# Half a weight chunk kept resident in place of a second output-tail buffer, in a streamed recurrent attention kernel

## The chip, the cores and the metric

The kernel runs on one core of one Trainium2 chip. The metric is the device time of one execution in microseconds. A time given here is the median of the fast runs of one kernel. A ratio is the mean time of one kernel's fast runs over the mean of the other's fast runs of the same rounds on the same chip, so it is not quite the ratio of the medians quoted beside it. All runs of this study were in the fast state. The kernel before was run anew beside each group of experiments, with medians from 2193 to 2199 us.

Names used below: PE is the matmul engine (TensorE), DVE the vector, ACT the scalar and POOL the general engine; SP issues the loads. The granted clock is the share of TensorE's full clock that the profile's records show. "The fill" is the copy of the memory rows into the input of a segment, once per segment.

## The reference, cut to what matters

The program computes two things side by side: a long convolution (part A, not touched here), and an attention with a recurrent memory (part B). Part B goes through 64 segments of 32 rows. Each segment takes eight memory rows from the output of the one before, so the segments cannot overlap.

```python
mem = mem0
for s in range(n_seg):                                   # 64
    h = jnp.concatenate([mem, x[:, s*32:(s+1)*32]], axis=1)
    q, k, v = (jnp.einsum('btd,dhe->bhte', h, W) for W in (Wq, Wk, Wv))
    p = softmax(where(mask, q @ k^T * scale, -1e9))
    o = jnp.einsum('bhte,hed->btd', p @ v, Wo)
    mem = o[:, :M, :]                                    # M = 8
    outs.append(o[:, M:, :])
```

The weights Wq, Wk, Wv and Wo are 64 chunks of [128, 2048] bf16, 512 KB each. The kernel holds only part of them on the chip.

## The kernel before: the parts that matter

43 of the 64 chunks stay resident. 21 are "streamed", two of which are kept in spare PSUM after the first segment, so 19 loads of 512 KB go through a ring of six slots in every segment. A load is issued only when a slot comes free: `done` of a used chunk calls `fetch`.

```python
def fetch():
    if loads:
        s, ch = loads.pop(0)
        live[s, ch] = k, t = slot()
        nc.sync.dma_start(t[:], stream_src(ch))

def done(ch):
    if ch in streamed:
        ...
        free.append(live.pop((now[0], ch))[0])
        ...                      # either a kept chunk is moved into the slot, or
        fetch()
```

The order of work in a segment (cut) is: K, Q and V projections for two groups of heads, scores, softmax, attention, output projection. Then comes the turn: eight rows of the result Y go through a transpose into the input of the next segment.

```python
k0 = Proj(0, 0).run().evac()
q0 = Proj(1, 0).run(4)
...                                        # KT0, QT0, k1
scores(0, QT0, KT0); softmax_a()
q1 = Proj(1, 1).run(4)
...
PT0 = softmax_b()                          # P_pad on DVE, transposed into PT
...
QT1 = one.tile(..., tag="QT"); nc.scalar.copy(QT1[:], transposes(q1))
scores(1, QT1, KT1); softmax_a()
...
out_proj(...)                              # with tail heads on streamed chunks
nc.scalar.copy(Y[:], yacc[:, 0:256])
if tail is not None and not last: tail.run(TURN[0])      # six heads as filler
if not last: fill_mem(pend[s + 1][0], Y)                 # the turn
...
if tail is not None and not last: tail.run(TURN[1])      # four more
```

The "tail" is the output projection of eight more rows per segment. They are collected in OTB for a pair of segments and multiplied together: 32 heads of four matmuls for each pair, then one store YB. A head whose output chunk is streamed has to ride along while that chunk is in the ring ("inline").

Of the kernel before, what the change touches and what calls it, by code (L numbers as in the profile page):

```python
# [9 lines left out]
BF = mybir.dt.bfloat16  # L10
F32 = mybir.dt.float32
# [11 lines left out]
KEPT = {18: "A", 6: "B"}  # L23
TURN = (6, 4)
INLINE = {1: 0, 3: 1, 5: 0, 11: 1, 12: 0, 14: 1}
N2, N3 = 12, 19
# [358 lines left out]
def b_kernel(ctx: ExitStack, tc, x, mem0, Wq, Wk, Wv, Wo, outb, n_seg, run_a):  # L385
    nc = tc.nc
    SEG = 32
    NX = 24
    NB = 2
# [9 lines left out]
    order = []  # L399
# [7 lines left out]
    streamed = set()  # L407
# [13 lines left out]
    def dram_chunk(ch):  # L421
        m, a, g = ch
        return Wo_v[a] if m == 3 else W_v[m][a, g]
# [4 lines left out]
    def stream_src(ch):  # L428
        return WS[ring_order.index(ch), :, 0:2048]
# [186 lines left out]
    one = ctx.enter_context(tc.tile_pool(name="b_one", bufs=1, side="right", reuse_waits="tile"))  # L616
    two = ctx.enter_context(tc.tile_pool(name="b_two", bufs=2, side="right", reuse_waits="tile"))
    ps_acc = ctx.enter_context(tc.tile_pool(name="b_ps_acc", bufs=2, space=PSUM))
# [15 lines left out]
    tacc = SB[:, 200:456]  # L634
# [14 lines left out]
    def slot():  # L649
        k = free.pop(0)  # L650
        t = ring.tile([128, 2048], BF, tag=f"wring{k}", name="wring")
        return k, t

    def fetch():
        if loads:
            s, ch = loads.pop(0)
            live[s, ch] = k, t = slot()
            nc.sync.dma_start(t[:], stream_src(ch))

# [12 lines left out]
    def pieces(ch):  # L672
        if ch in res:
            return [(0, 2048, res[ch])]
        t = live[now[0], ch][1]
        if kept.get(ch) == "B" and now[0] > 0:
            return [(0, 768, WB[:]), (768, 2048, t[:, 768:2048])]
        return [(0, 2048, t[:])]
# [7 lines left out]
    def done(ch):  # L686
        if ch in streamed:
# [7 lines left out]
            else:  # L695
                fetch()

    P_pad = one.tile([128, 5, 64], BF, name="P_pad")
    nc.vector.memset(P_pad[:], 0.0)

# [17 lines left out]
    with tc.manual_schedule():  # L718
# [17 lines left out]
        class Tail:  # L736


            def __init__(self, OTB, b, acc=None):
                self.OTB, self.b, self.acc = OTB, b, tacc if acc is None else acc  # L740
                self.seeded = acc is None
                self.left = list(range(32))
                nc.vector.memset(self.acc, 0.0)  # L743

            def head(self, h, w):
                g, c, i = h // 16, (h % 16) // 4, h % 4
                first = len(self.left) == 32
                self.left.remove(h)
                for dq in range(4):
                    o = (h % 2) * 1024 + dq * 256  # L750
                    for x, y, r in columns(w, o, o + 256):
                        nc.tensor.matmul(self.acc[32 * dq:32 * dq + W, x - o:y - o],  # L752
                                         lhsT=self.OTB[:, c, 4 * g + i, :], rhs=r,
                                         start=first and not self.seeded, stop=not self.left,
                                         skip_group_check=True, tile_position=(0, 32 * dq))
                if not self.left:
                    self.store()
# [5 lines left out]
            def store(self):  # L763
                YB = one.tile([128, 256], BF, tag="QT", name="YB")
                nc.vector.tensor_copy(YB[:], self.acc)  # L765
                for dq in range(4):
                    nc.gpsimd.dma_start(  # L767
                        bass.AP(outb.tensor, outb.offset + (SEG * NB * self.b + NX) * 2048 + 256 * dq,
                                [[2048 * SEG, NB], [2048, 8], [1, 256]]), YB[32 * dq:32 * dq + W, :])

        OTB = tail = own = None
        for s in range(n_seg):
            b, j = s // NB, s % NB
# [59 lines left out]

            def softmax_a():
                mx = two.tile([128, 5], F32, tag="mx", name="mx")
                nc.vector.tensor_reduce(out=mx[:], in_=S, op=ALU.max, axis=AX.X)  # L836
                nc.vector.tensor_tensor(out=S, in0=S, in1=mx[:].unsqueeze(2).to_broadcast([128, 5, 40]),
                                        op=ALU.subtract)
                nc.scalar.activation(S, S, ACT.Exp, scale=scale)

            def softmax_b():
                ssum = two.tile([128, 5], F32, tag="ssum", name="ssum")
                nc.vector.tensor_reduce(out=ssum[:], in_=S, op=ALU.add, axis=AX.X)  # L843
# [38 lines left out]
            def out_proj(hps, OT):  # L882
                for hp in hps:
                    ch = (3, hp, 0)
                    w = pieces(ch)
                    for hh in range(2):
                        h = 2 * hp + hh
                        g, c, i = h // 16, (h % 16) // 4, h % 4
                        for dq in range(4):
                            o = hh * 1024 + dq * 256  # L890
                            for x, y, r in columns(w, o, o + 256):
                                nc.tensor.matmul(yacc[32 * dq:32 * dq + 32, x - o:y - o], lhsT=OT[:, c, i, :],  # L892
                                                 rhs=r, start=(h == 0 and x == o), stop=(h == 31),
                                                 tile_position=(0, 32 * dq))
                    if tail is not None and 2 * hp in tail.left and (ch in streamed or last):
                        if last or INLINE[hp] == j:
                            tail.head(2 * hp, w)
                            tail.head(2 * hp + 1, w)
                    if own is not None and ch in streamed:
                        own.head(2 * hp, w)  # L900
                        own.head(2 * hp + 1, w)
                    done(ch)

            k0 = Proj(0, 0).run().evac()
            q0 = Proj(1, 0).run(4)
            KT0 = keys(0)
            last_queries(0)
            nc.vector.tensor_copy(KT0[:, :, :, 0:32], transposes(k0))  # L908
            q0 = q0.run(4).evac()
            k1 = Proj(0, 1).run(4)  # L910
            QT0 = one.tile([128, 4, 4, 32], BF, tag="QT", name="QT")
            nc.vector.tensor_copy(QT0[:], transposes(q0))
            k1 = k1.run(4).evac()
            scores(0, QT0, KT0)
            softmax_a()
            q1 = Proj(1, 1).run(4)
            KT1 = keys(1)
            last_queries(1)
            nc.scalar.copy(KT1[:, :, :, 0:32], transposes(k1))
            PT0 = softmax_b()  # L920
            q1 = q1.run(4).evac()
# [4 lines left out]
            scores(1, QT1, KT1)  # L926
            softmax_a()
            pv1 = Proj(2, 1).run(4)
            if j == 0:
                OTB_new = one.tile([128, 4, 8, 8 * NB], BF, tag=f"OTB{b % 2}", name="OTB")  # L930
                OTB = OTB_new
            attend(0, PT0, V0)
            OT0 = evac_o(0)
            PT1 = softmax_b()
            pv1.run(4)
# [3 lines left out]
            yacc = ps_acc.tile([128, 512], F32, tag="acc", name="yacc")  # L939
            if last:  # L940
                own = Tail(OTB, b, ps_acc.tile([128, 512], F32, tag="acc", name="own_acc")[:, 0:256])
            out_proj(range(0, 5), OT0)
# [5 lines left out]
            nc.scalar.copy(Y[:], yacc[:, 0:256])  # L948
            if j == NB - 1 and not last:
                tail = Tail(OTB, b)  # L950
            if tail is not None and not last:
                tail.run(TURN[0])
            if not last:
                fill_mem(pend[s + 1][0], Y)
            nc.gpsimd.dma_start(bass.AP(outb.tensor, outb.offset + SEG * s * 2048, [[256, 4], [2048, 32], [1, 256]]), Y[:])
            if tail is not None and not last:
                tail.run(TURN[1])
            if last:
                own.run(32)

# [69 lines left out]
```

## Time and profile before

Three runs gave 2200.15 us (2194.8 to 2205.34).

| Quantity | Value | Where from |
|---|---|---|
| Span of the profile | 2198.0 us | page |
| Rate in the segments | 383 to 393 GB/s | table of stretches |
| Granted TensorE clock, whole span | 0.965 | list of cores |

The lines themselves stand in the prediction. The table of stretches gives busy time for each engine, then the granted clock, the share of time the 16 DMA engines were busy with packets, and what they moved.

### The profile page before, as it was taken

The numbers are of one execution on the slowest core, as the hardware profiler recorded it, in microseconds if no ns is written. First come the engines' busy times: TensorE is split into PE (matmuls) and PEld (weight loads), VectorE is DVE, ScalarE is ACT, GpSimd is POOL, SyncE is SP. The second block draws the span as 40 slices with busy tenths as digits, with TensorE's granted clock in tenths as the row PEclk, the third lists the DMA queues.
The fourth block names the chain that finished last, engine by engine and source line by source line (L and its number), as shares of the span: only waits on it lengthen the run. The fifth ranks groups of instructions, "written<-read, shape, count | busy, mean of one in ns | idle before, by whom it ended". The sixth has DMA issues, their size and how long they took to land. (4 is left out here: it accounts for less than half of the span.)

```text
span 2198.0 us, 81500 instructions
## 1 busy us (share of the span) xinstructions
PE 1721.9 (78%) x35607; PEld 927.7 (42%) x35636; DVE 884.2 (40%) x2702; ACT 638.6 (29%) x1118; POOL 412.2 (19%) x1103
## 2 busy tenths in 40 slices
PE   4679975957777788878888888887887878888886
PEld 2233332424444444444444444444444444444444
DVE  8827853123333333333333333333333333333332
ACT  5845530112222222222222222222222222222222
POOL 5004331001111112111111111111111211211111
PEclk9889997879999999999999999999999999999999
DMA  9989989899999999999999999999999999999997
GB/s 322 345 291 342 318 238 325 275 346 390 386 380 378 381 374 390 385 378 395 391 392 395 391 393 393 392 397 365 396 392 387 394 390 376 388 392 388 390 385 273
DMA packets 294286, 807.80 MB, mean 368 GB/s; under 512 B 84940, under 2 KB 84972, under 8 KB 293927
## 3 DMA queue, kind: packets, MB, share of 16 engines
q1 hardware_dynamic: 263592, 738.36, 89.0%
q0 software_dynamic: 23536, 50.51, 6.8%
q10 hardware_dynamic: 6800, 13.72, 1.7%
q8 instruction: 279, 4.57, 0.9%
q14 instruction: 79, 0.65, 0.1%
HBM read 743.06 MB, written 62.39 MB: 366 GB/s over the span
## 5 line engine op out<-in xcount | busy, mean ns | idle before, releaser
L806 PEld LDWEIGHTS <-rec 128*32 128x32 bf16 x12351 | 324.2, 96 | 471.6 <-issue 255.0
L806 PE MATMUL acc<-wring,rec 128*32 128x512 bf16 (+1 forms) x3777 | 374.7, 385 | 136.0 <-DMA wring<-WS 122.1
L815 ACT CAST qkv_sb<-acc 128x512 bf16<-128x512 f32 x384 | 224.8, 585 | 676.2 <-PE acc L806 645.7
L806 PE MATMUL acc<-Wres,rec 128*32 128x512 bf16 x4864 | 394.9, 383 | 1.5 <-issue 1.4
L892 PEld LDWEIGHTS <-OT 128*32 128x32 bf16 x8192 | 217.8, 96 | 178.1 <-issue 151.6
L892 PE MATMUL yacc<-Wlate,OT 128*32 128x256 bf16 x5120 | 221.8, 274 | 13.0 <-issue 11.9
L892 PE MATMUL yacc<-wring,OT 128*32 128x256 bf16 x3072 | 153.9, 276 | 98.5 <-DMA wring<-WS 59.0
L806 PE MATMUL acc<-Wmid,rec 128*32 128x512 bf16 x3072 | 226.1, 383 | 0.5 <-issue 0.5
L752 PEld LDWEIGHTS <-OTB 128*16 128x16 bf16 x4096 | 104.5, 89 | 103.9 <-issue 94.0
L878 ACT CAST OT<-OTp 128x512 bf16<-128x512 f32 x128 | 74.9, 585 | 241.4 <-PE OTp L870 241.3
L707 POOL DMA_DIRECT2D rec<-REC x64 | 37.4, 584 | 566.6 <-issue 268.9
L908 DVE COPY KT<-tps 128x512 bf16<-128x512 bf16 x64 | 27.2, 424 | 289.1 <-PE tps L821 289.1
L879 DVE CAST OTB<-OTp 128x128 bf16<-128x128 f32 x128 | 37.3, 291 | 258.6 <-ACT OT L878 258.6
L647 DVE TENSOR_SCALAR wring<-OTp 128x384 int32<-128x384 int32 x126 | 112.2, 890 | 61.5 <-PE acc L806 54.2
L752 PE MATMUL SB<-Wlate,OTB 128*16 128x256 bf16 x2480 | 98.0, 277 | 35.4 <-DVE SB L743 19.3
L782 POOL COPY KT<-rec 128x128 bf16<-128x128 bf16 x128 | 38.6, 302 | 439.2 <-PE SB L830 430.9
L836 DVE TENSOR_REDUCE mx<-SB 128x5 f32<-128x200 f32 x128 | 47.1, 368 | 182.8 <-PE SB L830 182.8
L767 POOL DMA_DIRECT2D out_dram<-YB x128 | 73.1, 578 | 236.4 <-DVE YB L765 212.9
L752 PE MATMUL SB<-wring,OTB 128*16 128x256 bf16 x1488 | 78.8, 274 | 36.5 <-DVE SB L731 30.8
L821 PE MATMUL tps<-ident,qkv_sb 128*128 128x128 bf16 x1024 | 101.2, 221 | 7.8 <-DVE wring L647 0.2
L821 PEld LDWEIGHTS <-qkv_sb 128*128 128x128 bf16 x1024 | 62.7, 97 | 104.7 <-ACT qkv_sb L815 64.4
L556 PE MATMUL kb_ps<-XBT,pw 128*128 128x512 bf16 x314 | 87.7, 400 | 9.3 <-ACT XBT L512 7.6
(214 smaller groups left out, 2300.8 us busy)
## 6 DMA issues: line engine op xcount, KB each, us to landing
wring<-WS SPq DMA_DIRECT2D x1218, 512.0 KB, 7.3
rec<-REC POOLq DMA_DIRECT2D x64, 192.0 KB, 6.0
SK<-s_sb SPq DMA_DIRECT2D x16, 512.0 KB, 4.8
SU<-s_sb SPq DMA_DIRECT2D x16, 512.0 KB, 4.6
Ug<-SU SPq DMA_DIRECT2D x32, 256.0 KB, 6.1
Kg<-SK ACTq DMA_DIRECT2D x32, 256.0 KB, 5.5
REC<-stage SPq DMA_DIRECT2D x4, 2048.0 KB, 15.2
SZ<-zs SPq DMA_DIRECT2D x31, 256.0 KB, 3.0
```

The lines of the kernel that those rows point to most:

```text
L556: nc.tensor.matmul(ps[:], lhsT=ws[kc][:, hl * 128:(hl + 1) * 128], rhs=XBT[:, kc].rearrange("p s t -> p (s t)"), start=(kc == 0), stop=(kc ...
L647: nc.vector.tensor_scalar(out=dst, in0=src, scalar1=0, scalar2=None, op0=ALU.bitwise_or)
L707: nc.gpsimd.dma_start(rec[:], REC[:, s, :])
L752: nc.tensor.matmul(self.acc[32 * dq:32 * dq + W, x - o:y - o], lhsT=self.OTB[:, c, 4 * g + i, :], rhs=r, start=first and not self.seeded, ...
L767: nc.gpsimd.dma_start(bass.AP(outb.tensor, outb.offset + (SEG * NB * self.b + NX) * 2048 + 256 * dq, [[2048 * SEG, NB], [2048, 8], [1, 256 ...
L782: nc.gpsimd.tensor_copy(KT[:, :, :, 32:40], KBs[:, 128 * g:128 * g + 128].rearrange("p (c i t) -> p i c t", c=4, i=4))
L806: nc.tensor.matmul(self.acc[32 * c:32 * c + 32, x - 512 * c:y - 512 * c], lhsT=hT[:, kc, :], rhs=r, start=(kc == 0 and x == 512 * c), stop ...
L815: nc.scalar.copy(sb[:], self.acc[:])
L821: nc.tensor.transpose(tp[:, i * 128:(i + 1) * 128], sb[:, i * 128:(i + 1) * 128], ident[:])
L836: nc.vector.tensor_reduce(out=mx[:], in_=S, op=ALU.max, axis=AX.X)
L878: nc.scalar.copy(OT[:], o_view[:, :, :, 0:32])
L892: nc.tensor.matmul(yacc[32 * dq:32 * dq + 32, x - o:y - o], lhsT=OT[:, c, i, :], rhs=r, start=(h == 0 and x == o), stop=(h == 31), tile_po ...
```

## The change

The intent is to stream less. The left half of one K chunk (place 3 of the 64) becomes resident. Its 2 KB per partition come from one OTB buffer instead of two, from single buffers for two small softmax tiles, and from letting P_pad borrow the slots of the transposed Q and K. With one OTB, the tail of a pair must be finished before the next pair writes OTB, so the tail work moves: twelve heads inline in the second segment of each pair, ten as filler there, ten early in the next. YB moves from the slot "QT" to the slot "PT". The core of the diff:

```diff
-TURN = (6, 4)
-INLINE = {1: 0, 3: 1, 5: 0, 11: 1, 12: 0, 14: 1}
+TURN = (4, 6)
+HALF = 3
...
+    half = order[HALF]
+    WH = one.tile([128, 1024], BF, name="WH")
+    nc.gpsimd.dma_start(WH[:], dram_chunk(half)[:, 0:1024])
...
-            nc.sync.dma_start(t[:], stream_src(ch))
+            c = slice(1024 if ch == half else 0, 2048)
+            nc.sync.dma_start(t[:, c], stream_src(ch)[:, c])
...
-    P_pad = one.tile([128, 5, 64], BF, name="P_pad")
-    nc.vector.memset(P_pad[:], 0.0)
...
-                YB = one.tile([128, 256], BF, tag="QT", name="YB")
+                YB = one.tile([128, 256], BF, tag="PT", name="YB")
...
+            def softmax_a(g):
+                P_pad = one.tile([128, 5, 64], BF, tag="KT" if g else "QT", name="P_pad")
+                nc.gpsimd.memset(P_pad[:, 0:4, 32:64], 0.0)
...
-                        if last or INLINE[hp] == j:
+                    if j == NB - 1 and ch in streamed:
...
             k0 = Proj(0, 0).run().evac()
+            more_tail(4)
             q0 = Proj(1, 0).run(4)
+            more_tail(3)
...
             q0 = q0.run(4).evac()
+            more_tail(32)
...
-                OTB_new = one.tile([128, 4, 8, 8 * NB], BF, tag=f"OTB{b % 2}", name="OTB")
+                OTB = one.tile([128, 4, 8, 8 * NB], BF, tag="OTB", name="OTB")
```

More of the change, by code (lines that the diff above doesn't have):

```diff
@@ L616, in b_kernel @@
     one = ctx.enter_context(tc.tile_pool(name="b_one", bufs=1, side="right", reuse_waits="tile"))
-    two = ctx.enter_context(tc.tile_pool(name="b_two", bufs=2, side="right", reuse_waits="tile"))
+    two = ctx.enter_context(tc.tile_pool(name="b_two", bufs=1, side="right", reuse_waits="tile"))
     ps_acc = ctx.enter_context(tc.tile_pool(name="b_ps_acc", bufs=2, space=PSUM))
@@ L675, in pieces @@
         t = live[now[0], ch][1]
+        if ch == half:
+            return [(0, 1024, WH[:]), (1024, 2048, t[:, 1024:2048])]
         if kept.get(ch) == "B" and now[0] > 0:
@@ L736, in b_kernel, with __init__ @@
         class Tail:
-            def __init__(self, OTB, b, acc=None):
-                self.OTB, self.b, self.acc = OTB, b, tacc if acc is None else acc
-                self.seeded = acc is None
+            def __init__(self, OTB, b):
+                self.OTB, self.b, self.acc = OTB, b, tacc
                 self.left = list(range(32))
@@ L746, in head @@
                 g, c, i = h // 16, (h % 16) // 4, h % 4
-                first = len(self.left) == 32
                 self.left.remove(h)
@@ L753, in head @@
                                          lhsT=self.OTB[:, c, 4 * g + i, :], rhs=r,
-                                         start=first and not self.seeded, stop=not self.left,
+                                         start=False, stop=not self.left,
                                          skip_group_check=True, tile_position=(0, 32 * dq))
@@ L769, in store @@
                                 [[2048 * SEG, NB], [2048, 8], [1, 256]]), YB[32 * dq:32 * dq + W, :])
-        OTB = tail = own = None
+        OTB = tail = None
         for s in range(n_seg):
@@ L832, in scores @@
                                          tile_position=(0, 32 * c))
-            def softmax_a():
+            def softmax_a(g):
+                P_pad = one.tile([128, 5, 64], BF, tag="KT" if g else "QT", name="P_pad")
+                nc.gpsimd.memset(P_pad[:, 0:4, 32:64], 0.0)
                 mx = two.tile([128, 5], F32, tag="mx", name="mx")
@@ L839, in softmax_a, with softmax_b @@
                 nc.scalar.activation(S, S, ACT.Exp, scale=scale)
-            def softmax_b():
-                ssum = two.tile([128, 5], F32, tag="ssum", name="ssum")
+                return P_pad
+            def softmax_b(P_pad):
+                ssum = two.tile([128, 5], F32, tag="mx", name="ssum")
                 nc.vector.tensor_reduce(out=ssum[:], in_=S, op=ALU.add, axis=AX.X)
@@ L894, in out_proj, with more_tail @@
                                                  tile_position=(0, 32 * dq))
-                    if tail is not None and 2 * hp in tail.left and (ch in streamed or last):
-                        if last or INLINE[hp] == j:
-                            tail.head(2 * hp, w)
-                            tail.head(2 * hp + 1, w)
-                    if own is not None and ch in streamed:
-                        own.head(2 * hp, w)
-                        own.head(2 * hp + 1, w)
+                    if j == NB - 1 and ch in streamed:
+                        tail.head(2 * hp, w)
+                        tail.head(2 * hp + 1, w)
                     done(ch)
+            def more_tail(n):
+                if tail is not None and j == 0:
+                    tail.run(n)
             k0 = Proj(0, 0).run().evac()
+            more_tail(4)
             q0 = Proj(1, 0).run(4)
+            more_tail(3)
             KT0 = keys(0)
@@ L914, in b_kernel @@
             scores(0, QT0, KT0)
-            softmax_a()
+            P0 = softmax_a(0)
             q1 = Proj(1, 1).run(4)
@@ L919, in b_kernel @@
             nc.scalar.copy(KT1[:, :, :, 0:32], transposes(k1))
-            PT0 = softmax_b()
+            PT0 = softmax_b(P0)
             q1 = q1.run(4).evac()
@@ L926, in b_kernel @@
             scores(1, QT1, KT1)
-            softmax_a()
+            P1 = softmax_a(1)
             pv1 = Proj(2, 1).run(4)
             if j == 0:
-                OTB_new = one.tile([128, 4, 8, 8 * NB], BF, tag=f"OTB{b % 2}", name="OTB")
-                OTB = OTB_new
+                OTB = one.tile([128, 4, 8, 8 * NB], BF, tag="OTB", name="OTB")
             attend(0, PT0, V0)
             OT0 = evac_o(0)
-            PT1 = softmax_b()
+            PT1 = softmax_b(P1)
             pv1.run(4)
@@ L939, in b_kernel @@
             yacc = ps_acc.tile([128, 512], F32, tag="acc", name="yacc")
-            if last:
-                own = Tail(OTB, b, ps_acc.tile([128, 512], F32, tag="acc", name="own_acc")[:, 0:256])
+            if j == NB - 1:
+                tail = Tail(OTB, b)
             out_proj(range(0, 5), OT0)
@@ L948, in b_kernel @@
             nc.scalar.copy(Y[:], yacc[:, 0:256])
-            if j == NB - 1 and not last:
-                tail = Tail(OTB, b)
-            if tail is not None and not last:
+            if j == NB - 1:
                 tail.run(TURN[0])
@@ L955, in b_kernel @@
             nc.gpsimd.dma_start(bass.AP(outb.tensor, outb.offset + SEG * s * 2048, [[256, 4], [2048, 32], [1, 256]]), Y[:])
-            if tail is not None and not last:
-                tail.run(TURN[1])
-            if last:
-                own.run(32)
+            if j == NB - 1:
+                tail.run(32 if last else TURN[1])
 @with_exitstack
```

## The prediction

> **What bounds the kernel now.** I read the page's slices first, then the table of stretches, the chain of waits, the list of waits and a timeline of one segment. The kernel has two stages. Up to about 460 us it does the convolution and preparation; after that come 64 sequential segments, and only those are changed. The fill of the memory rows happens once per segment; its first copy starts at 468.6 us and the last at 2159.1 us, so a segment takes (2159.1 - 468.6) / 63 = 26.83 us. In each segment 19 chunks of 512 KB are streamed into a six-slot ring (1218 loads in all). Two stretches inside the segments, columns: length, busy us (instructions) of PE, PEld, DVE, ACT, POOL, then granted clock, DMA share, GB/s:
>
> ```profile
> 1000.00:1400.00 400.00, 325.72 (x8073) 186.20 (x8069) 146.88 (x529) 104.54 (x198) 72.14 (x227) 1.00 1.02 393
> 1400.00:1800.00 400.00, 324.02 (x7961) 184.95 (x7957) 145.69 (x524) 102.44 (x194) 69.90 (x223) 0.99 1.01 389
> ```
>
> The DMA engines are full (share 1.0) at 389 to 393 GB/s. PE is busy for 81% and idle for (400 - 325.72) / 400 x 26.83 = 5.0 us of a segment. The chain of waits, asked for 1900 to 1965 us, says the same: what releases a load is the slot freed by the matmuls of an earlier load, and most of the chain is the transfer itself.
>
> ```profile
> by line: DMA wring<-WS 86.8%; PE acc L806 6.3%; PE yacc L892 5.9%; DVE wring L647 4.0%; issue 2.3%; PE tps L821 1.2%; PE SB L752 1.0%; DVEq L912 0.1%; PE SB L830 0.1%; PE SB L827 0.1%; DVEq L647 0.0%
> ```
>
> How much room PE has is in the waits (us in total, times, longest). PE waits for the stream 122.1 + 59.0 = 181 us, 2.8 us a segment; the rest of its 5.0 us is latency of softmax, copies and the recurrence.
>
> ```profile
> PE acc L806 <- DMA wring<-WS: 122.1, 276, 2.0
> PE yacc L892 <- DMA wring<-WS: 59.0, 110, 1.6
> PE SB L752 <- DVE SB L731: 30.8, 29, 1.6
> PE SB L752 <- DVE SB L743: 19.3, 28, 0.7
> ```
>
> The buffer between both is in the list of issues (KB, us to landing): a load lands 7.3 us after its issue because some six are in flight, so PE may fall several us behind before the DMA engines run out of requests. The small stores take almost as long[...]:
>
> ```profile
> wring<-WS SPq DMA_DIRECT2D x1218, 512.0 KB, 7.3
> out_dram<-Y POOLq DMA_DIRECT2D x64, 64.0 KB, 6.4
> out_dram<-YB POOLq DMA_DIRECT2D x128, 8.0 KB, 5.0
> ```
>
> [...] the packet records have a median of 162 ns for the 163,712 packets of 4096 B on the ring's queue and 84 ns for those of 2048 B (26,907 on the same queue, all of the first stage), 3.7% more per byte. [...] The trace shows 393 GB/s here[...] and I use the measured rate. [...]
>
> **The change, part by part.**
>
> Half a chunk resident. Columns 0 to 1023 of the fourth K chunk stay in SBUF; the ring fetches only the other half, 128 packets of 2048 B in place of 128 of 4096 B. On 16 engines that is 128 x (162 - 84) ns / 16 = 0.624 us less per segment, 64 x 0.624 = 39.9 us in all. By bytes alone, 262144 B at 393 GB/s would be 0.667 us and 42.7 us; the shorter packet takes the difference back. It is paid once with the resident half's own load, 128 x 84 / 16 = 0.67 us of engine time in the crowded start. Matmul forms do not change, since the cut at 1024 lies between two 512-column matmuls. As the DMA engines set the pace, this part should come through nearly whole: -39 us.
>
> The output tail. A pair of segments still does 32 tail heads with 128 matmuls, about 0.11 us of PE per head at the measured 8 matmuls in 0.22 us. Before: each segment runs six heads inline and ten as filler around the recurrence. After: twelve inline and ten filler in the second segment of a pair, the other ten early in the next segment, where PE waits for transposes or the stream. PE work is moved, not removed. The wait on L743 (19 us) should go, because the accumulator is cleared long before its first matmul; the one on L731 stays, at one segment of each pair. PE is not the bound, so I count 0.
>
> The end. The last segment had two tails: the store of the first held the slot that the second needed, and the program ended 12.6 us after its last Y copy (2185.4 to 2198.0). Now one tail is left; its YB shares a slot with Y and waits for Y's store alone. I estimate -2 us.
>
> P_pad in the Q and K slots. It adds 128 memsets of 128x128 on POOL, about 0.3 us each by the KT copy of that size (302 ns), off the path. It also makes the copy of the second Q wait until softmax has transposed P_pad out of the first Q's slot; in the timeline that was done at 1024.1 us and the copy began at 1025.6 us, so there is 1.5 us of room.
>
> YB in the slot of PT. This is the new cost. YB is now copied about 7.5 us into the first segment of each pair, after the last tail head; four stores of 0.56 us follow on POOL, the last starting 1.7 us later and landing 5.0 us after that: about 14.5 us into the segment. The transposes that fill PT need this slot. Before they began 10.6 us after the fill in this segment:
>
> ```profile
> 1012.99 0.19 DVE L714 COPY rec<-tps 128x64 bf16<-128x64 bf16 x1 [1.20 <-issue]
> 1023.54 0.30 DVE L857 STREAM_TRANSPOSE PT<-P_pad 128x128 bf16<-128x128 bf16 x1
> 1025.60 0.58 ACT L924 COPY QT<-tps 128x512 bf16<-128x512 bf16 x1 [0.94 <-PE tps L821]
> ```
>
> So DVE should stand about 3.5 us for YB's landing in 31 or 32 segments, and PE some 2 to 3 us at the second scores, because the copy of Q waits for P_pad. During that stand about two chunks land, with three or more still on order: the DMA engines stay fed. PE must then make it up: of the 2.8 us of waiting for the stream, 0.6 goes to the faster stream and at most 3.3 / 2 = 1.65 us a segment on average to this stall, which leaves some 0.5 us. That is thin, so I charge 5 us, about 0.15 us per pair, for stretches where PE runs late.
>
> Sum: 2200 - 39 - 2 + 5 = 2164 us.
>
> **The rivals.** First, the stall makes PE the bound: 3 us in 32 pairs is 96 us of PE time. If none could be made up, the 39 us would be lost and the kernel would be slower; against it stands the 5.8 us of stream waits per pair. If a third is not made up, 32 us of the gain goes and the time is about 2190. Second, everything is hidden and the shuffle of tail work also removes bubbles: the stretches before vary between 371 and 393 GB/s, and if the new order held the upper end throughout, some 10 us more would come, about 2150. Third, the DMA engines gain less than the packet times say, because the freed slot waits for something else (DVE moving a kept chunk into the ring, 112 us in all) and the stream idles: about 2175.
>
> **Range and chances.** The upper bound of the gain without new luck is 41 us, to 2159; the 2% line is 0.98 x 2200 = 2156. Before itself spread over 10 us. So faster by over 2% needs the second rival: 0.15. Slower by over 2% needs the whole first one: 0.03. Within 2%: 0.82. Eight in ten: 2150 to 2185.
>
> **What would show it.** Right: the segment falls from 26.83 to about 26.2 us with a DMA share still at 1.0; a new wait of DVE's PT for the stores of YB, 60 to 130 us in total, 31 or 32 times; PE's waits for the stream fall from 181 us to under 120. Wrong: a DMA share under 0.98 in the segments (PE became the bound), first segments of a pair longer by more than a us than second ones with the time not regained, or loads of 256 KB whose packets take clearly more than 84 ns.

## The result

The changed kernel took 2259.08 us (2249.71 to 2277.09, four runs) against 2197.48 us. The ratio is 1.0285, 95% interval 1.0214 to 1.0355: slower, where a gain of 36 us had been predicted. The pairs of segments became longer, from 53.70 us to 55.86 us on average between fills.

First the same two stretches of the changed kernel's segments, with the same columns as in the prediction:

```profile
1000.00:1400.00 400.00, 316.81 (x7555) 178.39 (x7554) 139.57 (x501) 97.98 (x187) 72.57 (x244) 0.94 0.97 361
1400.00:1800.00 400.00, 316.89 (x7749) 179.49 (x7748) 141.90 (x513) 99.03 (x189) 72.39 (x240) 0.96 0.98 367
```

The rate is 361 to 367 GB/s where it had been 389 to 393. That is a loss of 7%, while only 2.5% fewer bytes have to be moved. The DMA share fell to 0.97 and 0.98. PE is less busy too, and its granted clock is lower.

The issues of the changed kernel show that the loads themselves are as intended: 64 of them are half as large.

```profile
wring<-WS SPq DMA_DIRECT2D x1154, 512.0 KB, 7.2
wring<-WS SPq DMA_DIRECT2D x64, 256.0 KB, 7.1
```

The waits of the changed kernel (us in total, times, longest):

```profile
ACT QT L932 <- DVE PT L863: 112.7, 31, 5.8
DVE PT L862 <- DMA out_dram<-YB: 110.7, 31, 4.6
PE acc L808 <- DMA wring<-WS: 102.7, 198, 2.3
...
PE SB L829 <- ACT QT L932: 70.0, 31, 4.6
...
PE SB L754 <- DVE SB L746: 47.4, 32, 1.7
...
DVE rec L718 <- DMA rec<-REC: 46.7, 14, 4.3
...
PE yacc L897 <- DMA wring<-WS: 27.9, 59, 1.4
```

The wait on YB's store is there as predicted: 31 times, 3.6 us each. Behind it wait the copy of QT and PE's second scores. PE still waits for the stream, 102.7 us in the projections against 122.1 before; the waits in the output projection fell further, from 59.0 to 27.9 us. A wait on the load of the next segment's rows (L718) is new: that load is issued only when the delayed V projection has freed its tile. PE's wait for that fill grew with it, to 24.4 us; it is 9.2 us in yb_own, a run below without the stall.

One such stall, from the chain that ended last in the changed kernel (start, length, what):

```profile
1028.26 0.42 DVE YB L767
...
1028.97 1.62 POOL out_dram L769 x3
...
1030.68 5.84 DMA out_dram<-YB
...
1036.64 0.31 DVE PT L862
...
1037.44 0.60 ACT QT L932
...
1038.08 0.20 PE SB L829 x4
```

YB is copied at 1028.26, its four stores are issued until about 1031.2, and the last lands at 1036.5. Only then may DVE overwrite PT, ACT copy Q and PE go on.

Three causes were possible: the stall by itself (theory S), the rearranged tail work (rival C), or something about the half-size load (rival P).

### The profile page after: what moved, and what is told of

It is laid out like the page before. It is cut to its first block, busy times and chain, and to the rows that moved or that the text cites. A ratio compares the mean times of both kernels' runs of the same rounds, so it can differ in the third digit from the quotient of the medians.

```text
span 2259.2 us, 81979 instructions
## 1 busy us (share of the span) xinstructions
PE 1739.9 (77%) x35607; PEld 930.0 (41%) x35636; DVE 884.6 (39%) x2701; ACT 635.9 (28%) x1118; POOL 436.9 (19%) x1232
## 4 chain that ended last, share of the span: by engine, by line
DMA 47%; PE 33%; DVE 8%; issue 4%; ACT 4%; POOL 1%; SPq 1%; DVEq 0%; ACTq 0%; POOLq 0%
DMA wring<-WS 32%; PE acc L808 12%; DMA out_dram<-YB 6%; PE yacc L897 5%; PE kb_ps L556 4%; PE SB L754 4%; DVE wring L647 3%; PE vb_ps L598 2%; DMA rec<-REC 2%; ACT OT L883 1%; ACT s_sb L210 1%; PE tps L823 1%; DVE PT L862 1%; DMA SU<-s_sb 1%; POOL out_dram L769 1%
## 5 line engine op out<-in xcount | busy, mean ns | idle before, releaser
L808 PE MATMUL acc<-wring,rec 128*32 128x512 bf16 (+1 forms) x3649 | 390.2, 398 | 134.7 <-DMA wring<-WS 102.7
L808 PE MATMUL acc<-Wres,rec 128*32 128x512 bf16 x4864 | 418.0, 398 | 4.1 <-issue 4.0
L897 PE MATMUL yacc<-Wlate,OT 128*32 128x256 bf16 x5120 | 231.8, 283 | 15.0 <-issue 14.7
L808 PE MATMUL acc<-Wmid,rec 128*32 128x512 bf16 x3072 | 234.6, 396 | 3.9 <-issue 3.9
L897 PE MATMUL yacc<-wring,OT 128*32 128x256 bf16 x3072 | 159.6, 283 | 62.9 <-DVE wring L647 28.0
L838 POOL MEMSET P_pad<- 128x128 bf16 x128 | 26.8, 210 | 605.3 <-PE SB L832 605.3
L960 POOL DMA_DIRECT2D out_dram<-Y x64 | 46.1, 721 | 464.4 <-ACT Y L955 450.0
L754 PE MATMUL SB<-wring,OTB 128*16 128x256 bf16 x1536 | 84.6, 286 | 49.8 <-DVE SB L746 47.4
L862 DVE STREAM_TRANSPOSE PT<-P_pad 128x128 bf16<-128x128 bf16 x256 | 73.2, 286 | 110.8 <-DMA out_dram<-YB 110.7
L754 PE MATMUL SB<-Wlate,OTB 128*16 128x256 bf16 x2560 | 103.8, 275 | 10.7 <-issue 10.7
```

The source lines that it names most:

```text
L754: nc.tensor.matmul(self.acc[32 * dq:32 * dq + W, x - o:y - o], lhsT=self.OTB[:, c, 4 * g + i, :], rhs=r, start=False, stop=not self.left, ...
L808: nc.tensor.matmul(self.acc[32 * c:32 * c + 32, x - 512 * c:y - 512 * c], lhsT=hT[:, kc, :], rhs=r, start=(kc == 0 and x == 512 * c), stop ...
L862: nc.vector.transpose(out=PT[:, kb, :, 0:32], in_=P_pad[:, 0:4, ks])
L897: nc.tensor.matmul(yacc[32 * dq:32 * dq + 32, x - o:y - o], lhsT=OT[:, c, i, :], rhs=r, start=(h == 0 and x == o), stop=(h == 31), tile_po ...
L960: nc.gpsimd.dma_start(bass.AP(outb.tensor, outb.offset + SEG * s * 2048, [[256, 4], [2048, 32], [1, 256]]), Y[:])
```

## The experiments

Several kernels read a wrong chunk on purpose to get memory for a test. The comparison with the reference has a tolerance, and some of these still passed it; they are not valid versions all the same. The diffs are cut.

### One part alone

**half_only**: the kernel before, with the half-size load and nothing else.

```diff
+            c = slice(1024 if ch == half else 0, 2048)
+            nc.sync.dma_start(t[:, c], stream_src(ch)[:, c])
...
+        if ch == half:
+            return [(0, 1024, res[order[2]][:, 0:1024]), (1024, 2048, t[:, 1024:2048])]
```

> The kernel before with the half-size load alone: the ring fetches only columns 1024 to 2047 of the fourth K chunk, and the matmuls of the first half read a resident chunk in its place, so no memory is needed and the result is wrong on purpose. Theory S (the new stall of softmax on the store of YB, never made up, is what costs): this part is good by itself, about 2160 us, ratio 0.98 to 0.985, DMA share 1.0. Rival P (2 KB packets or the odd load size slow the stream): 2200 us or more, and packets of 2048 B well over 84 ns. Rival C (bunched tail work): 2160 as well.

Measured: 2192.41 us, ratio 0.998 (0.9937 to 1.0023). No theory had this: the load is harmless, but the 39 us that were the purpose of the change are not there. About 4 us are, not clear of noise (the interval runs from a gain of 14 us to a loss of 5). The packets are not to blame: the records give a median of 84 ns for the 2048 B ones, exactly as assumed.

**tail_only**: everything of the change except the half chunk.

```diff
-    WH = one.tile([128, 1024], BF, name="WH")
-    nc.gpsimd.dma_start(WH[:], dram_chunk(half)[:, 0:1024])
...
-            c = slice(1024 if ch == half else 0, 2048)
+            c = slice(0, 2048)
```

> The changed kernel with the whole chunk streamed again: everything of the change but the half chunk. Theory S: the stall, not the stream, sets the pace, so the time stays near the changed kernel's 2259 us, 2245 to 2290. Rival P: back to about 2200 us. Rival C: as S.

Measured: 2270.29 us, ratio 1.0348. The loss lies in the rest of the change, and rival P falls. Inside the changed kernel the half chunk is worth about 11 us by the medians (2270 less 2259) and 14 by the ratios.

**yb_own**: the changed kernel with a slot of its own for YB.

```diff
-    WH = one.tile([128, 1024], BF, name="WH")
-    nc.gpsimd.dma_start(WH[:], dram_chunk(half)[:, 0:1024])
+    WH = res[order[2]][:, 0:1024]
...
-                YB = one.tile([128, 256], BF, tag="PT", name="YB")
+                YB = one.tile([128, 256], BF, tag="YB", name="YB")
```

> The changed kernel with a slot of its own for YB; the room comes from not holding the half chunk, whose matmuls read a resident chunk instead (wrong on purpose). Theory S: the wait of PT for YB's stores is gone and the time falls to 2160 to 2180 us, granted clock back near 0.965. Rival C (the tail's work bunched into every second segment, P_pad in borrowed slots): stays above 2235 us. Rival P: stays at 2255 us.

**yb_late**: the changed kernel, valid, with YB stored later from a slot that is free for long.

```diff
-                if not self.left:
+                if not self.left and last:
                     self.store()
...
-                YB = one.tile([128, 256], BF, tag="PT", name="YB")
+                YB = one.tile([128, 256], BF, tag="QT", name="YB")
...
             out_proj(range(5, 8), OT0)
+            if tail is not None and j == 0:
+                tail.store()
```

> The changed kernel, right results, all of its memory saving kept, but YB is stored later: in the middle of the output projection of the first segment of a pair, from the first Q slot, which nobody needs until some 10 us into the next segment. Theory S: 2160 to 2180 us, with no wait on the stores of YB over 1 us. Rival C: above 2235 us. Rival P: about 2255 us.

Measured: yb_own 2214.49 us (1.0093), yb_late 2209.46 us (1.0066). Taking the stall away gives back 45 to 50 us of the 62 (42 to 48 by the ratios). So theory S holds for the larger part. But both runs miss the 2160 to 2180 us, because half_only shows that there was nothing to fall to, and both stay above half_only by some 20 us.

### What the stream really does

half_only needs an explanation: 2.5% fewer bytes and no time gained. I looked at its stretches:

```profile
1000.00:1400.00 400.00, 328.46 (x8086) 187.88 (x8076) 147.96 (x529) 103.54 (x196) 72.89 (x229) 0.99 1.01 385
1400.00:1800.00 400.00, 321.83 (x7921) 185.48 (x7921) 145.49 (x523) 102.80 (x194) 69.15 (x222) 0.99 0.99 378
```

The share is still about 1.0, yet the rate is 378 to 385 GB/s. So a mean share of 1.0 over many segments does not mean that no more can be moved. I had read the share alone. In four stretches from 500 to 2150 us it was 1.00 to 1.02 at 383 to 393 GB/s in the kernel before, and 0.99 to 1.01 at 375 to 385 in half_only.

From the records of packets (all queues) I worked out the rate in each us after the fill of a segment's memory rows, the mean of 55 segments, in GB/s:

```
us after the fill   0   1   2   3   4   5   6 |  7-22 (mean) | 23  24  25  26
before            365 361 344 335 351 365 379 |  402         | 400 392 369 373
half_only         334 324 309 321 343 361 375 |  403         | 386 348 329 347
half_mid          359 351 322 322 345 361 385 |  398         | 400 374 369 374
```

In the middle of a segment the stream runs at 402 GB/s. Around the turn it does not. The likely reason is in the times of the ring's loads, on average in the kernel before: the load of place 3 is issued 6.5 us ahead of the fill, and the next one (place 7) only 3.1 us ahead, because its slot comes free late in the output projection. A shorter load of place 3 lands about 0.3 us earlier, and then nothing follows it sooner: place 7 is issued 3.1 us ahead of the fill in half_only too. Against 403 GB/s, summed over the eleven us outside the middle, the kernel before leaves 399 KB unmoved around each turn and half_only 656 KB: 257 KB more, and the load was 262 KB smaller. That about the whole saving is unmoved follows from the unchanged time; what the table adds is that it all lies around the turn.

Read by phase and not as a mean, the share shows it too. In the middle of a segment it is 1.02 in both kernels. In the four us after the fill it is 0.96 to 0.99 before and 0.89 to 0.97 in half_only, and in the last three us of the table 0.99 to 1.01 against 0.90 to 0.95. Not all of the dip before is idling: 2 to 4 us after the fill the share is 0.98 to 1.00, while a packet of 4096 B takes 178 to 184 ns on average instead of about 164. What slows the packets there was not tested.

**thin_before** and **thin_after** fetch every streamed chunk of segments 1 to 63 by half.

```diff
+            c = slice(1024 if s > 0 else 0, 2048)
+            nc.sync.dma_start(t[:, c], stream_src(ch)[:, c])
...
+        if now[0] > 0 and ch not in kept:
+            return [(0, 1024, t[:, 1024:2048]), (1024, 2048, t[:, 1024:2048])]
```

> The kernel before with every streamed chunk of segments 1 to 63 fetched by half and its right half used for both (wrong on purpose): the same instructions, matmuls and waits, about 48% fewer bytes in the segments. If the rate of the DMA engines set the pace (what the prediction said), the pace of PE's own chain shows and the time falls far, under 2060 us. Theory L (the pace is set by the loop of PE's order of work, latencies and the six slots, with the DMA engines just about keeping up): it falls only a little, 2120 to 2185 us.

> The changed kernel with every streamed chunk fetched by half in the same way. If its stall only costs because the stream then falls behind, it comes down to the thin kernel before, within 1%. Theory L with the stall inside PE's chain: it stays 40 to 70 us above the thin kernel before, with the waits on the stores of YB still there but shorter[...].

Measured: 1948.85 us (0.8871) and 2021.8 us (0.9209). The stream does cost 250 us in all, so my theory L in its strong form (PE's chain sets the pace) falls. The kernel before is bound by the rate in one part of a segment and by latency and slots in the other. The second run matters for the stall. The stretch 1000 to 1400 us of the thin kernel before, then of the thin changed one:

```profile
1000.00:1400.00 400.00, 351.78 (x9339) 207.00 (x9342) 171.32 (x616) 121.38 (x230) 84.31 (x269) 1.00 0.75 238
```

```profile
1000.00:1400.00 400.00, 341.31 (x8841) 199.71 (x8834) 162.35 (x583) 114.68 (x219) 84.88 (x283) 0.97 0.71 225
```

And two waits of the thin changed kernel:

```profile
DVE PT L864 <- DMA out_dram<-YB: 58.3, 29, 3.5
PE SB L831 <- ACT QT L934: 52.8, 30, 3.3
```

With the DMA engines at 0.7, far from full, the change still costs 73 us. So the stall and the moved work lie in the chain of one segment after the other, and do not act by way of a stream that falls behind. The stores land sooner beside the smaller stream: an 8 KB store of YB landed 5.0 us after its issue in the kernel before and 5.5 us in the changed one, against 3.2 and 3.5 us in the two thin ones. Why it takes that long was not tested.

**ring7**: the kernel before with a seventh slot.

```diff
-RING = 6
+RING = 7
...
+    res[late[-1]] = res[parts[0][0]]
-    for i, ch in enumerate(late):
+    for i, ch in enumerate(late[:-1]):
```

> The kernel before with a seventh ring slot, its memory taken from one resident output chunk whose matmuls read another (wrong on purpose). If six slots are too few (latency of a load against PE's uneven use), the time falls by 20 us or more. If the rate of the DMA engines is the bound, or PE's chain, it stays within 8 us of before.

Measured: 2177.11 us, ratio 0.9908 (0.9871 to 0.9944). It moves the same bytes and gains about 20 us. A stretch and the ring's loads in it:

```profile
1000.00:1400.00 400.00, 323.45 (x8017) 186.44 (x8010) 146.91 (x525) 103.76 (x196) 71.80 (x230) 1.00 1.02 393
```

```profile
wring<-WS SPq DMA_DIRECT2D x1218, 512.0 KB, 8.5
```

In this stretch the rate equals that of the kernel before; from 600 to 2100 us it is 391.9 against 387.7 GB/s. A load lands 8.5 us after its issue instead of 7.3: one more is in flight. So slots, not only bytes, are short.

**half_mid**: half_only with another chunk, place 43, which is loaded in the middle (diff against half_only).

```diff
-    half = order[3]
+    half = order[43]
```

> As the half-size load alone, but of another chunk: the fourth V chunk of the second half of the heads (place 43 of 64 instead of 3), first half read from a resident chunk, wrong on purpose. Theory W (where the load lies decides: chunk 3 is loaded around the turn from one segment to the next, where the records show 300 to 360 GB/s because slots come free late, while chunk 43 is loaded where the stream runs at 400 GB/s without a gap): the gain appears, 20 to 40 us, 2160 to 2180 us. If a smaller load helps nowhere (the loop of slots counts loads, not bytes): 2190 us again.

Measured: 2171.47 us, ratio 0.9878 (0.9849 to 0.9907). The same number of bytes saved at another place is worth about 27 us by the ratio (24 by the medians) in place of 4, some two thirds of the 39 us. PE's waits for the stream in half_only and then in half_mid:

```profile
PE acc L811 <- DMA wring<-WS: 125.3, 254, 1.9
PE yacc L897 <- DMA wring<-WS: 58.8, 109, 1.7
```

```profile
PE acc L811 <- DMA wring<-WS: 82.3, 198, 1.6
PE yacc L897 <- DMA wring<-WS: 64.3, 113, 1.9
```

In half_only PE waits as long for the stream as before (122.1 and 59.0 us). In half_mid 43 us of the wait in the projections are gone.

### What the moved tail costs

**own_both**: yb_own with a slot of its own for P_pad too, so that only the half-size load and the new order of the tail remain.

```diff
+    P_pad = one.tile([128, 5, 64], BF, name="P_pad")
+    nc.vector.memset(P_pad[:], 0.0)
...
-                P_pad = one.tile([128, 5, 64], BF, tag="KT" if g else "QT", name="P_pad")
-                nc.gpsimd.memset(P_pad[:, 0:4, 32:64], 0.0)
```

> The changed kernel with slots of their own for YB and for P_pad (its memory from not holding the half chunk, wrong on purpose): what is left of the change is the order of the tail's work and the half-size load. If P_pad's borrowed slots and the 128 memsets cost, it falls from 2214 to about 2192 us, as the half-size load alone did. If the order of the tail costs, it stays at 2205 to 2220 us with a granted clock of about 0.945.

Measured: 2213.02 us, ratio 1.0073 (1.0043 to 1.0104), against 1.0093 (1.0054 to 1.0132) for yb_own. P_pad in borrowed slots costs at most some us. The new order of the tail costs about 20 us: 2213 against 2192 for half_only.

**no_inline_old** and **no_inline_new** leave out the tail heads that ride on streamed chunks, in the old order (six in each segment) and in the new one (twelve in every second). Both have the half-size load of place 3 and a slot of its own for YB; P_pad has its own slot only in the new one.

```diff
-                self.left = list(range(32))
+                self.left = [h for h in range(32) if (3, h // 2, 0) in res]
...
-                    if j == NB - 1 and ch in streamed:
-                        tail.head(2 * hp, w)
-                        tail.head(2 * hp + 1, w)
```

> Control for the order of the tail, wrong on purpose: the old order with two output-tail buffers and the half-size load of place 3, but without the tail heads that ride on the streamed output chunks (six in each segment); YB in its own slot, P_pad in borrowed slots. Less PE work in the turn of every segment: 2150 to 2185 us, granted clock 0.96.

> The new order with one output-tail buffer, slots of their own for YB and P_pad, the half-size load, and without the twelve tail heads that ride on the streamed output chunks of every second segment, wrong on purpose. If it is those twelve in one segment that cost the 20 us of the new order, it comes within 8 us of the old order without them. If it is the rest of the new order (no filler at the turn after first segments, ten heads early in the next), it stays 15 us or more above. The clock shows in which part the lower grant comes from: near 0.96 or still 0.947.

Measured: 2148.92 us (0.9801) and 2155.22 us (0.9809). The difference between the orders shrinks from 0.9 to 0.1 points. So it is the twelve heads in one segment that cost, their wait for the clearing (next run) included. They lie in the output projection, just ahead of the turn. PE's waits for the stream there, split by segment, fit this: 22 us in first and 37 us in second segments before, 59 and 14 us in own_both. The heads left the first segments, where PE now stands for the stream, and crowd the second ones. The inline heads cost about 43 us in the old order (2192 less 2149), and some 58 us in the new one (2213 less 2155), for the same number of matmuls. At the prediction's 0.11 us a head, twelve heads in 32 pairs are 42 us of PE time: even in the old order next to none of it was hidden.

**early_clear**: own_both with the tail's accumulator cleared earlier.

```diff
             P1 = softmax_a(1)
+            if j == NB - 1:
+                tail = Tail(OTB, b)
...
-            if j == NB - 1:
-                tail = Tail(OTB, b)
             out_proj(range(0, 5), OT0)
```

> The new order with slots of their own for YB and P_pad (2213 us as measured), and the tail's accumulator cleared before the second softmax finishes instead of after it. If the wait of the first tail head on that clearing (44 us in total, 1.4 us each) is what costs, 2195 to 2205 us; if not, 2209 to 2216 us.

Measured: 2205.05 us, ratio 1.0051 (1.0028 to 1.0075), at the edge of what was expected if that wait mattered. By the ratios that is 0.2 points less than own_both, some 5 us, and the two intervals overlap. PE's wait ahead of the first tail head, in own_both and then in early_clear:

```profile
PE SB L756 <- DVE SB L748: 43.8, 32, 1.5
```

```profile
PE SB L756 <- DVE SB L737: 30.5, 31, 1.1
```

The wait only got shorter by 13 us in total: it passes to the seeding of the scores in the same bank, which the kernel before also waits for. Some 5 to 8 us of the new order's 20 probably went with it. The time at half clock speed (next section) also fell, from 102 to 59 us, so wait and clock are not separated here.

### The clock

Most kernels with the new order had a lower granted clock: 0.940 in the changed kernel and 0.947 in own_both, against 0.964 in half_only; early_clear, with 0.963, is the exception. The changed kernel's stretches around one wait of PE, cut at the borders of the clock records (same columns). The wait is that of a first tail head for the clearing, 1.5 us in a second segment, not the stall on YB:

```profile
1066.11:1069.53 3.42, 1.46 (x48) 1.13 (x47) 2.12 (x12) 0.58 (x1) 0.60 (x1) 1.00 1.02 405
1069.53:1072.94 3.41, 3.41 (x96) 2.25 (x92) 1.52 (x2) 0.59 (x1) 0.00 (x0) 0.50 1.03 401
1072.94:1076.35 3.41, 3.02 (x94) 2.18 (x86) 0.00 (x0) 0.37 (x1) 0.00 (x0) 1.00 0.68 202
```

PE is busy for 1.46 of 3.42 us in the first, runs at half speed (granted clock 0.50) for the 3.41 us of the second, and in the third the stream has dropped to 202 GB/s. From the first fill to the end the changed kernel has 39 such periods, 31 of them of this length; the stretch of this length ahead of one had a median of 2.0 us without a matmul, and 1.7 us at the least. Over the same time the records show 161 us at half speed in the changed kernel, 32 us before, 43 us in half_only and 102 us in own_both.

**after_warm** and **own_warm** keep the waits and fill them with idle matmuls.

```diff
+            pv1 = Proj(2, 1)
+            for _ in range(16 if j == 0 and s > 0 else 0):
+                nc.tensor.matmul(pv1.acc[:, 0:256], lhsT=ident[:], rhs=res[order[2]][:, 0:256],
+                                 start=True, stop=True, skip_group_check=True)
             scores(1, QT1, KT1)
```

```diff
+                        for _ in range(12 if hp == 1 else 0):
+                            nc.tensor.matmul(yacc[:, 256:512], lhsT=ident[:], rhs=WARM, start=False, stop=False,
+                                             skip_group_check=True)
                         tail.head(2 * hp, w)
```

> The changed kernel with 16 idle matmuls (128x256, results overwritten, about 1.8 us) in front of the second scores of every first segment, where PE stands for the store of YB anyway. The stall on YB stays as long as it was. If the half-speed windows that follow a stall (161 us of the segments in the changed kernel, 32 us in the one before) are part of the cost, half-speed time falls to about 100 us and the time by 8 to 30 us, to 2230 to 2250. If the stall costs by its length alone, the time stays at 2255 us or rises.

> The new order with slots of their own for YB and P_pad (2213 us), with 12 idle matmuls (128x256 into unused columns) in front of the first inline tail head of every second segment, where PE stands 1.4 us for the clearing of the accumulator. Clock theory: half-speed time in the segments falls from 102 to about 60 us and the time by 3 to 12 us. If the wait costs by its length alone: 2211 us or more, as idle matmuls cannot shorten it.

The 1.8 us for 16 idle matmuls are an estimate: in the trace of the kernel before, matmuls of 128x512 (L556) started 0.216 us apart (median), which makes about 1.7 us for 16 of half as many columns.

Measured: after_warm 2249.51 us, ratio 1.025 (1.0216 to 1.0285); own_warm 2211.29 us, ratio 1.0087 (1.0061 to 1.0114). The clock did what was intended: half-speed time fell from 161 to 111 us and from 102 to 73 us. The time did not follow clearly. The first gained perhaps 8 us, within the intervals; the second nothing (its ratio is 0.1 points higher). YB's wait in after_warm is unchanged:

```profile
DVE PT L862 <- DMA out_dram<-YB: 114.1, 31, 4.8
```

So the part of the half-speed time that was taken away, 50 and 29 us, was worth little. The rest was not tested, and idle matmuls also take PE time (about 1.7 us for 16 by the estimate above) where a wait happens to be short. For the stall there is a bound: in yb_own, without it, the profiled run is 38 us shorter while the half-speed time fell only from 161 to 137 us. At half rate at most half of these 24 us can have been lost, an estimate of 12 us from the two traces, so the stall costs mainly by its length. For the order of the tail there is none: own_both has 58 us more at half speed than half_only, up to 29 us by the same estimate, and its whole cost is 20 us.

### Versions that keep the memory and avoid the losses

**late_mid**: yb_late with the resident half taken from place 43 (`HALF = 43`), valid.

> The changed kernel with right results, YB stored late as in the earlier run, and the resident half taken from place 43 instead of 3. Theory W: 15 to 35 us under the late store alone (2209 us), so 2175 to 2195 us, and faster than before. If the place does not matter: 2209 us.

Measured: 2194.68 us, ratio 0.9989 (0.9958 to 1.002). The place is worth 15 us here too, and the version is no slower than before. But it was expected to be faster, and it is not; what is left of the loss is about the size of the new order's cost.

**quarter512**: the kernel before with both OTB buffers and the old tail. Only P_pad and the small tiles give up memory, and that buys 512 resident columns of chunk 43. It is valid.

```diff
+    half = order[43]
+    WH = one.tile([128, 512], BF, name="WH")
+    nc.gpsimd.dma_start(WH[:], dram_chunk(half)[:, 0:512])
...
-    P_pad = one.tile([128, 5, 64], BF, name="P_pad")
-    nc.vector.memset(P_pad[:], 0.0)
...
+                P_pad = one.tile([128, 5, 64], BF, tag="KT" if g else "QT", name="P_pad")
+                nc.gpsimd.memset(P_pad[:, 0:4, 32:64], 0.0)
```

> A version without the new order of the tail, right results: the kernel before with two output-tail buffers, P_pad in the Q and K slots, and in the memory that this frees 512 columns of chunk 43 resident (a quarter). Theory W with the order of the tail as the remaining cost: a quarter of a chunk is worth 10 to 20 us, so 2178 to 2190 us, granted clock 0.96. If P_pad in borrowed slots costs: 2200 us or more.

Measured: 2184.11 us, ratio 0.9948 (0.9915 to 0.998). Half as many bytes saved, and the only valid version here that is faster than before beyond its interval, though by half a per cent.

## Why the prediction was wrong

Point by point, by its own steps:

- **"As the DMA engines set the pace, this part should come through nearly whole: -39 us."** This is the first step that failed. The sizes were right (84 ns packets, 262 KB less in each segment), the place was not asked for. Chunk 3 is loaded around the turn, where slots come free late, and there half_only gave 4 us. The same load in the middle gave 27 us (half_mid). The prediction took a mean DMA share of 1.0 as proof that the rate binds everywhere; half_only has a share that rounds to the same (0.996 against 1.012, 600 to 2100 us) at 2.4% less rate.
- **The stall of DVE on YB.** Right in its size: "about 3.5 us", "31 or 32 segments", PE 2 to 3 us at the second scores, a total of "60 to 130 us". It was 3.6 us, 31 times, 2.3 us at PE (70.0 / 31), 110.7 us.
- **"PE must then make it up ... so I charge 5 us".** This is the second step that failed, and the largest. The stall cost 45 to 50 us (2259 against 2214 and 2209). The prediction counted all 2.8 us of stream waits of a segment as room; in all they fell by 50 us, from 181 to 131. Where the time went shows in the traces of yb_own and the changed kernel, which differ in the stall and the half load's source. In the first segments the 70 us that PE stood at the second scores did take 63 us out of its stream waits (105 to 43 us). But other waits of PE grew by some 40 us: 11 us more for the stream in second segments, 13 for the fill there, 9 for DVE moving a kept chunk into the ring, and smaller ones. The room was there, and the time came back later in the chain. That a full stream is not needed for this shows thin_after, where the change costs 73 us. The first rival, "If a third is not made up", came nearest; net of all, 45 to 50 us were not made up.
- **"PE work is moved, not removed ... so I count 0."** This is the third that failed: 20 us. The same matmuls cost more when twelve heads stand in one segment ahead of its turn, and PE's time for them was not free in either order (no_inline_old). Nor did the wait for the clearing go, as predicted ("should go", 19 us): it is 47.4 us in the changed kernel (L746), since DVE reaches the clearing only after the second softmax (at 1068.26 us in one segment, where PE had stood for 1.51 us).
- **P_pad in borrowed slots.** Right that it costs little: own_both and yb_own differ by less than their intervals. A memset took 0.21 us, not 0.3.
- **The end.** The last copy of Y to the end took 11.6 us (2247.56 to 2259.2) instead of 12.6: 1 us, not 2.
- **Its signs.** The DMA share fell under 0.98 (0.973, 600 to 2100 us), but not because PE became full: PE was busy for 79% of the stretches shown, against 81%. The stream waits stayed above 120 us. In the traces, first segments grew by 1.5 us to 27.8 and second ones by 0.7 us to 28.1, so first ones did not become the longer ones.
- **Two small readings.** 181 us are 5.7 us of stream waits per pair, not 5.8. The 371 GB/s of the second rival belongs to a stretch that runs past the last segment; inside the segments the lowest was 378.

In ratios to the kernel before: -0.2 points for the half load (half_only), +0.9 for the order of the tail (own_both), +0.2 for P_pad, inside the intervals (yb_own), +1.9 for YB in PT's slot (the changed kernel). They add up to the measured 2.8 by construction, since each is the step from one kernel to the next. In another order the parts differ: the half load is worth 0.6 points when it is taken out of the changed kernel (tail_only).

Still open is how much of this is the half-speed clock: some 12 us at most of the stall's cost by the estimate above, and anything up to the whole of the tail's.

## What to carry to other kernels

A stream can be short of rate in one part of a loop and short of free slots in another, and a mean DMA share of 1.0 hides this: in the kernel before it was 1.012, with 402 GB/s in the middle of a segment and 335 to 379 in the seven us after the fill. Before saving bytes, look at rate and share over the phase of the loop, and save where the rate stands at its top: the same saving was worth about 27 us there and 4 us around the turn. A stall that fills waits has not been paid for if the same waits, or others, come back later in the chain; here 45 to 50 us were not made up. When a tile borrows the slot of another, ask when its store will have landed (5.5 us after its issue here), and give stores the slot that is next needed latest: YB in PT's slot gave 2259 us, stored later from the slot of QT 2209 us.
